# Attention and two feed-forward layers on one core: the first pass's input matmul in f16 parts, sums of |x| for the scales, one ring of streamed weights

## The chip, the core and the metric

The kernel runs on one core of a Trainium2 chip. The metric is device time in microseconds (us) of a whole execution. The engines are TensorE (PE, matmuls, with its weight loads PEld), VectorE (DVE), ScalarE (ACT), GpSimd (POOL), and the queue of SyncE (SP), which issues the DMA transfers. Each engine takes its instructions in program order, so an instruction that waits holds all that stand behind it on that engine.

## The reference

Four batches, eight heads, 576 positions and 64 dimensions a head give 2304 tokens of 512 columns. A position attends to all positions of its own and of earlier blocks of 64. Two feed-forward layers follow, 512 to 2048 to 512 columns, the first with h * tanh(softplus(h)) (Mish), the second with the square of relu.

```
attn = softmax(where(block_i >= block_j, q @ k.T / 8, -1e9));  x = attn @ v
h = x @ moe_w_in;   x = (h * tanh(log1p(exp(h)))) @ moe_w_out
h = maximum(x @ moe2_w_in, 0);   out = (h * h) @ moe2_w_out
```

## The kernel before

The tokens are cut into six chunks of 384. A pass is one layer of one chunk, and the twelve passes run in the order (layer, chunk) = (0,0), (0,1), (0,2), (1,0), (1,1), (0,3), (1,2), (1,3), (0,4), (0,5), (1,4), (1,5). The attention of a later chunk is laid beside the passes of earlier ones: `attention_lo` (chunks 0 and 1, f32 matmuls, tiles of 192) and `attention_hi` (chunks 2 to 5, f16 parts, scores at L903, maximum at L914, exponential at L925, product at L1011).

A pass takes eight weight pairs j, each two columns f of 128 hidden units. The first matmul of a column is four steps over the 512 inputs into one of two PSUM banks `hp`; ACT turns the bank into `h` with Mish or relu; `g_parts` (L1116 to L1118 the high part, L811 the low one) cuts g into two f16 parts; the second matmul adds into four banks `acc`. In most passes f32 is imitated by f16 parts: three f16 matmuls (high x high, low x high, high x low) for a step, in `first_half` (L1343) and `second_half` (L1456). Four passes go by a scheme of seven products (`first_seven`, L1376). All this needs the scale of a chunk's x (`chunk_scale`: one matmul at L1268 over per-token maxima `xm`, then operations on single columns that end in `cst`), the parts `xt` of x cut with it (L1276), and the norm and the parts of each weight pair (`decode` L1135 to L1146, `weigh` L1158 and L1161, `split` L1176). Pass (0,0) alone multiplies in f32, with `first_full` (L1407) and `second_full` (L1421). It needs no scale of x and no parts, only the decoded pairs; layer 0's w_in pairs are split later, out of the f32 pairs that lie in the buffer `first`.

The maxima of |x| that the scales start from are DVE reductions (L1028 in `settle`, L1428, L1473, L1550). Sums of absolute values are taken elsewhere, by `absum`, on ACT (L822) or DVE. An ACT function may need a table load first; the tasks carry a `table` by which the planner counts that, and those of `absum` carry none.

Layer weights that are not kept are written to `wspill` and read back by `weights` (L1246) into rings of buffers: `ws` up to pass 2, `wl` from pass 3, `wm` from pass 8. `wl` lies in the same memory as `ws`, and one line (L1747) makes its first three loads wait for all uses of `ws`:

```
    follow(R["wl"].insts[0:3], R["ws"].insts)
```

The order of the whole program is a table of numbers, `PLAN`, decoded by `Sched.planned`: for each place in the order it gives a task and the engine that runs it (tasks made by `choose` may run on one of several). The table was found by a search over a planner's estimates, and with the table the planner's estimates no longer matter.

## Time and profile before

| what | value |
|---|---|
| median of three runs | 898.1 us (894.83 to 899.0) |
| the profiled execution | 896.62 us, of which the span from first to last instruction is 894.8 |
| PE busy | 866.2 us, 97% |
| DVE busy | 766.5 us, 86% |
| ACT busy | 606.8 us, 68% |
| POOL busy | 54.2 us, 6% |
| first step on PE of passes 1 and 3 | 131.5 and 297.1 us |

The shares are means over the span. The windows of the section of rows cut it at the passes: a number in brackets there counts instructions, PEclk is the granted clock of TensorE as a share of full speed, and the DMA share is the mean busy share of the core's 16 DMA engines. A line such as L811 belongs to a helper and stands for several uses, told apart by the tile's name.

### The profile page before, as it was taken

The numbers are of one execution on the slowest core, as the hardware profiler recorded it, in microseconds if no ns is written. First come the engines' busy times: TensorE is split into PE (matmuls) and PEld (weight loads), VectorE is DVE, ScalarE is ACT, GpSimd is POOL, SyncE is SP. The second block draws the span as 40 slices with busy tenths as digits, with TensorE's granted clock in tenths as the row PEclk, the third lists the DMA queues.
The fourth block names the chain that finished last, engine by engine and source line by source line (L and its number), as shares of the span: only waits on it lengthen the run. The fifth ranks groups of instructions, "written<-read, shape, count | busy, mean of one in ns | idle before, by whom it ended". The sixth has DMA issues, their size and how long they took to land.

```text
span 894.8 us, 18486 instructions
## 1 busy us (share of the span) xinstructions
PE 866.2 (97%) x7034; PEld 600.7 (67%) x7034; DVE 766.5 (86%) x1816; ACT 606.8 (68%) x1157; POOL 54.2 (6%) x62
## 2 busy tenths in 40 slices
PE   7999999979999999999999999999999999999997
PEld 6664545545555456555556577777787877799997
DVE  6888988979989788886999899999887887689876
ACT  6799999899778675566678898975454333356332
POOL 1000100101110001000000000000010001010000
PEclk9999999999999999999999999999999999999999
DMA  9996676988798899588989699998569474766751
GB/s 340 362 354 263 167 158 174 246 260 292 250 300 206 187 242 224 180 195 216 218 261 277 244 215 264 257 236 319 196 247 335 162 287 173 257 215 236 249 200 59
DMA packets 162777, 213.02 MB, mean 238 GB/s; under 512 B 107392, under 2 KB 125824, under 8 KB 162688
## 3 DMA queue, kind: packets, MB, share of 16 engines
q1 hardware_dynamic: 162688, 211.84, 79.0%
q8 instruction: 55, 0.90, 0.4%
q14 instruction: 34, 0.28, 0.1%
...
## 4 chain that ended last, share of the span: by engine, by line
PE 71%; DVE 11%; ACT 9%; DMA 6%; issue 3%; SPq 0%; DVEq 0%; ACTq 0%
PE acc L1456 22%; PE hp L1376 15%; PE hp L1343 11%; PE acc L1496 4%; PE hp L1407 4%; PE acc L1421 3%; PE bank L903 3%; PE bank L1011 2%; DMA late<-pb 2%; DMA arena<-wspill 2%; PE bank L1496 2%; DVE st L914 1%; DVE pb L811 1%; ACT vs L822 1%; ACT pad L925 1%
## 5 line engine op out<-in xcount | busy, mean ns | idle before, releaser
L1456 PE MATMUL acc<-g,arena 128*128 128x384 f16 x1560 | 299.5, 326 | 0.1
L1456 PEld LDWEIGHTS <-arena 128*128 128x128 f16 x1560 | 147.2, 98 | 87.3 <-issue 4.6
L1343 PE MATMUL hp<-xt,first 128*128 128x384 f16 x576 | 111.3, 326 | 5.0 <-ACT h L1348 5.0
L1376 PEld LDWEIGHTS <-arena 128*128 128x128 f16 x1002 | 85.0, 98 | 13.5 <-DMA arena<-wspill 1.5
L1343 PEld LDWEIGHTS <-first 128*128 128x128 f16 x576 | 54.6, 98 | 44.8 <-issue 10.4
L811 DVE SCALAR_TENSOR_TENSOR g<-h,cst,g 128x768 f16<-128x768 f32 x72 | 73.2, 1017 | 3.1 <-ACT g L1116 2.5
L1343 PE MATMUL hp<-xt,arena 128*128 128x384 f16 x384 | 74.8, 332 | 0.9 <-DMA arena<-wspill 0.9
L925 ACT ACTIVATE pad<-bank,st,sq 128x448 f32<-128x448 f32 (+1 forms) x96 | 65.1, 681 | 13.9 <-DVE st L919 10.1
L811 DVE SCALAR_TENSOR_TENSOR pb<-pad,st,pb 128x384 f16<-128x384 f32 (+2 forms) x96 | 71.1, 749 | 2.6 <-ACT pb L945 2.5
L914 DVE TENSOR_REDUCE st<-bank 128x1 f32<-128x448 f32 (+1 forms) x96 | 53.2, 574 | 22.6 <-PE bank L906 14.4
L1348 ACT ACTIVATE h<-hp,cst 128x384 f32<-128x384 f32 x80 | 44.3, 576 | 29.6 <-PE hp L1343 28.9
L945 ACT ACTIVATE pb<-pad,st 128x640 f16<-128x640 f32 (+2 forms) x72 | 51.6, 725 | 14.6 <-DVE st L937 5.2
L1376 PEld LDWEIGHTS <-first 128*128 128x128 f16 x672 | 57.2, 98 | 5.2
L1376 PE MATMUL hp<-arena 128*128 128x192 f16 x534 | 55.2, 246 | 0.0
L1343 PEld LDWEIGHTS <-arena 128*128 128x128 f16 x384 | 36.7, 99 | 26.5 <-issue 2.8
L1397 ACT ACTIVATE h<-h,cst 128x576 f32<-128x576 f32 x32 | 24.7, 773 | 38.2 <-DVE h L1395 38.2
L1407 PE MATMUL hp<-xs,first 128*128 128x384 f32 x128 | 48.6, 492 | 1.0 <-ACT h L1411 1.0
L1376 PE MATMUL hp<-xt,arena 128*128 128x192 f16 x468 | 46.7, 246 | 1.2 <-DMA arena<-wspill 0.8
L1210 DVE TENSOR_TENSOR arena<-arena 128x256 f32<-128x256 f32 x96 | 40.6, 423 | 0.9
L903 PE MATMUL bank<-q 64*128 64x448 f16 (+2 forms) x384 | 39.3, 306 | 1.6 <-ACT xs L1025 0.7
L1116 ACT ACTIVATE g<-h,cst 128x768 f16<-128x768 f32 x36 | 33.5, 930 | 9.9 <-PE acc L1456 7.6
L1421 PE MATMUL acc<-h,late 128*128 128x384 f32 x96 | 37.4, 495 | 0.0
...
## 6 DMA issues: line engine op xcount, KB each, us to landing
...
arena<-in_w_dram SPq DMA_DIRECT2D x27, 1023.8 KB, 6.5
...
```

Source lines behind the costliest of these rows:

```text
L811: return sch.add("DVE", c_dve(n) + 62 * ap, lambda: nc.vector.scalar_tensor_tensor(dst(), a(), s() if ap else s, c(), op0, op1), r=r, w=w, ...
L903: nc.tensor.matmul(out=pp.t[hd][:, o:o + k1 - k0], lhsT=qh.t[rows, u, a:a + 128], rhs=qh.t[rows, w, nq + k0:nq + k1], start=p == 0, stop=p ...
L914: t = sch.add("DVE", c_dve(o1 - o0), lambda hd=hd: nc.vector.reduce_max(st.t[:, 2 * j + hd:2 * j + hd + 1], pp.t[hd][:, o0:o1], axis=AX.X) ...
L925: t = sch.add("ACT", c_act(o1 - o0, True, 3), lambda hd=hd: nc.scalar.activation(pf[hd].t[r0:, k0:k0 + o1 - o0], view(hd)[r0:, o0:o1], AF. ...
L945: "ACT": ("ACT", c_act(n, False, 1), lambda pb=pb, pv=pv, s=s: nc.scalar.activation(pb.t[:, 0:i + 1, 0, :], pv(), AF.Copy, scale=s()), False),
L1343: nc.tensor.matmul(out=hp.t[:, 0:n], lhsT=w.t[:, f % 2, a, 128 * k:128 * k + 128], rhs=x.t[:, c, k, 0:n], start=k == 0 and i == 0, stop=k ...
L1348: sch.add("ACT", c_act(n, True, 1), lambda f=f, o=o, hp=hp: nc.scalar.activation(h.t[:, o * n:o * n + n], hp.t[:, 0:n], (AF.Mish, AF.Relu) ...
L1376: nc.tensor.matmul(out=bank.t[:, o:o + z], lhsT=lhs, rhs=x.t[:, c, ks[k], :], start=start and k == 0 and i == 0, stop=k == 1 and i == 2, s ...
L1407: nc.tensor.matmul(out=hp.t[:, 0:n], lhsT=wf.t[:, 512 * (f % 2) + 128 * k:512 * (f % 2) + 128 * k + 128], rhs=xs.t[:, k, 0:n], start=k == ...
L1421: ts.append(sch.add("PE", c_mm(4 * n), lambda m=m, acc=acc: nc.tensor.matmul(out=acc.t[:, 0:n], lhsT=wf.t[:, 512 * (f % 2) + 128 * m:512 * ...
L1456: nc.tensor.matmul(out=acc.t[:, 0:n], lhsT=wo.t[:, f % 2, a, 128 * m:128 * m + 128], rhs=g.t[:, c, f % 2 * n:f % 2 * n + n], start=f == 0 ...
L1496: nc.tensor.matmul(out=acc[bank].t[:, o:o + c1 - c0], lhsT=lhs, rhs=g.t[:, c, z * b + c0:z * b + c1], start=j == 0 and (bank, o) in first ...
```

## The change

The first two weight pairs of pass (0,0) keep the f32 matmul (`NFULL` is 2); pairs 2 to 7 go through `first_half` with f16 parts. So chunk 0's x gets a scale and parts as well, in the buffer that chunk 2 uses later, and each w_in pair of layer 0 is normed by itself. The pairs from the third on are decoded into the ring `wf` of two buffers and split from there; the first two lie in the last two places of `first`. The rules that held a split back until the f32 readers were done are gone.

All maxima become `absum`, sums of |x|, in f32, on ACT or DVE; chunk 0 gets them too. `absum` tells the planner that it wants ACT's exponential table. The rings `ws` and `wl` become one, `ws`, used up to pass 7, and the line that made the first loads wait goes. The table `PLAN` is another one. Its order has 49 ACT table loads where the old has 58; 16 f32 steps of the first matmul in pass 0 where the old has 64; 26 norm matmuls (L1161) where there were 20, and 12 scale matmuls (L1268) where there were 11. Of the 56 sums of x 36 are on ACT and 20 on DVE, where 48 maxima were on DVE; DVE gets 24 more operations on single columns.

```diff
-X_AT = {(0, 1): "b", (0, 2): "c", (0, 3): "a", (0, 4): "y", (0, 5): "z",
+X_AT = {(0, 0): "c", (0, 1): "b", (0, 2): "c", (0, 3): "a", (0, 4): "y", (0, 5): "z",
...
-    "c-mE(34o8){{KJc`95YC!!UMHghWcHt0<L7`@SmIEvYL-S4pc#H>p%N+GtND>8DMLXc5`>-56sDV;{y?X3Y8gU*|l}^PT=pGxPmE=bX>^tnc^dGhZS`YDzOX"
...
+    "c-l>x2Vhji*2mB6-XydTO6Wz3C;}oXqJj-ju>gt)=zEGNs3<5RJXBEZiYWNm6%kQEd?<EQ#QGGF-g^(dg-$5RobNX?_Xb#Yv$=QX%qjo#Kj-X5q@1YcNL?w?"
...
-    R["wl"] = fixed([pair(arena[:, 1024 * i:1024 * i + 1024]) for i in range(3)])
...
     for j in range(NF // 2):
-        R["f32", 0, j] = fixed([first[:, 1024 + 2048 * j:3072 + 2048 * j].bitcast(F32)])
+        if j < NFULL:
+            R["f32", 0, j] = fixed([first[:, 2048 * (j + NF // 2 - NFULL):2048 * (j + NF // 2 - NFULL + 1)].bitcast(F32)])
         R["res", 0, 0, j] = fixed([first[:, 2048 * j:2048 * j + 2048].rearrange("p (a f c) -> p f a c", a=2, f=2)])
...
-    R["xm"] = sb("xm", [128, 8], BF16, 12)
+    R["xm"] = sb("xm", [128, 8], F32, 5)
+    junk = cp.tile([128, NX], BF16, name="junk")
+
+    nbytes[0] += 2 * NX
...
-    R["cst"] = sb("cst", [128, 37], F32, 4)
+    R["cst"] = sb("cst", [128, 37], F32, 3)
...
-    for key, old, more in (("wm", "wl", [pair(late[:, 0:1024]), pair(late[:, 1024:2048]), pair(vst[:, 1536:2560])]),
+    for key, old, more in (("wm", "ws", [pair(late[:, 0:1024]), pair(late[:, 1024:2048]), pair(vst[:, 1536:2560])]),
...
     def absum(n, total, src, spare, r, w):
...
-            "DVE": ("DVE", c_dve(n), lambda: nc.vector.tensor_reduce(total(), src(), axis=AX.X, op=ALU.add, apply_absolute_value=True), False)}, r, w)
+            "DVE": ("DVE", c_dve(n), lambda: nc.vector.tensor_reduce(total(), src(), axis=AX.X, op=ALU.add, apply_absolute_value=True), False)}, r, w).table = "exp"
...
-        xs, xm, whole = xs
+        xs, xm = xs
         dst = lambda: xs.t[:, k, xo:xo + n]
...
-        if not whole:
-            sch.add("DVE", c_dve(n), lambda: nc.vector.tensor_reduce(
-                xm.t[:, j:j + 1], dst(), axis=AX.X, op=ALU.max, apply_absolute_value=True), r=[(xs, (k, xo))], w=[(xm, j)])
+        absum(n, lambda: xm.t[:, j:j + 1], dst, lambda: junk[:, 0:n], [(xs, (k, xo))], [(xm, j)])
...
-    halves_of, used = {}, {}
...
     def decode(l, k, j):
 
         sch.group = "decode", l, k, j
         raw = R["raw2" if l else "raw"].new()
-        wf = (R["f32", k, j] if l == 0 else R["wf"]).new()
+        wf = R["wf" if l or not k and j >= NFULL else ("f32", k, j)].new()
...
-        if (l, k) == (0, 0):
-            hi = [t for t in w.tasks if t not in lo]
-            lo[0].deps.update(hi)
-            halves_of[j] = hi, lo
         if (k, j) in RES[l]:
...
-            w = fetched[pi, l, k, j] = R["wm" if pi >= WM_AT else "wl" if pi >= WL_AT else "ws"].new()
+            w = fetched[pi, l, k, j] = R["wm" if pi >= WM_AT else "ws"].new()
...
-    def chunk_scale(l, xs, xm, x, n, m, at, first, seven, lone):
+    def chunk_scale(l, xs, xm, x, n, m, at, seven, lone):
...
-        step = sch.add("PE", 120.0, lambda: nc.tensor.matmul(out=sc.t[:, 0:m], lhsT=ones, rhs=xm.t[:, 0:m], start=True, stop=True), r=[xm], w=[sc])
+        step = sch.add("PE", 120.0, lambda: nc.tensor.matmul(out=sc.t[:, 0:m], lhsT=ones, rhs=upper(xm.t[:, 0:m]), start=True, stop=True), r=[xm], w=[sc])
...
-        def spread():
-            for a, b in [(2 * j, 2 * j + 2) for j in range(NF // 2)] if first else [(0, NF)]:
+        def spread(j=None):
+            for a, b in [(0, NF) if j is None else (2 * j, 2 * j + 2)]:
                 tiny(lambda a=a, b=b: nc.vector.tensor_scalar(c(HS + a, b - a), st.t[:, IN + a:IN + b], c(PX), 0.25, ALU.mult, ALU.mult),
                      [(cst, PX)] + [(st, (0, j)) for j in range(a // 2, b // 2)], [(cst, (HS, j)) for j in range(a // 2, b // 2)], b - a)
...
-                sch.add("DVE", c_dve(n), lambda m=m, o=o: nc.vector.tensor_reduce(
-                    xm.t[:, m:m + 1], o(), axis=AX.X, op=ALU.max, apply_absolute_value=True), r=[(xs, (m, 0))], w=[(xm, m)])
+                absum(n, lambda m=m: xm.t[:, m:m + 1], o, lambda: junk[:, 0:n], [(xs, (m, 0))], [(xm, m)])
...
                 if l == 0:
-                    sch.add("DVE", c_dve(n), lambda m=m, o=o: nc.vector.tensor_reduce(
-                        xm.t[:, m:m + 1], o(), axis=AX.X, op=ALU.max, apply_absolute_value=True), r=dst, w=[(xm, m)])
+                    absum(n, lambda m=m: xm.t[:, m:m + 1], o, lambda: junk[:, 0:n], dst, [(xm, m)])
...
-                sch.add("DVE", c_dve(n), lambda m=m: nc.vector.tensor_reduce(
-                    xm.t[:, m:m + 1], y.t[:, m, 0:n], axis=AX.X, op=ALU.max, apply_absolute_value=True), r=r, w=[(xm, m)])
+                absum(n, lambda m=m: xm.t[:, m:m + 1], lambda m=m: y.t[:, m, 0:n], lambda: junk[:, 0:n], r, [(xm, m)])
...
+        xs, xm = whole(A_SLOT[c]), R["xm"].new()
         begin = len(sch.tasks)
-        place(chunk_steps(c, (xs, xm, c == 0), c < 2), a, b)
+        place(chunk_steps(c, (xs, xm), c < 2), a, b)
...
-    wfs, wos, m1s, hs = [], [], [], []
+    sch.group = "scale", 0, 0
+    x0, cst0, _, spread0, _, _ = chunk_scale(0, *source[0, 0], halved(X_AT[0, 0]), n, 8, A_AT[0][1], False, False)
+    sch.group = None
+    wfs, wos, hs, us0 = [], [], [], []
     for j in range(NF // 2):
         wfs.append(decode(0, 0, j))
         wos.append(decode(0, 1, j))
-        hs.append(R["h"].new())
+        us0.append(weigh(0, 0, [j], [wfs[j]], S_AT[0][0] + j * S_AT[0][1]))
+        if j < NFULL:
+            hs.append(R["h"].new())
+            m1 = [t for f in (2 * j, 2 * j + 1) for t in first_full(f, n, xs, wfs[j], hs[j])]
+            m1[0].mark = (0, 0) if j == 0 else None
+        else:
+            split(0, 0, j, wfs[j], us0[j], 0)
+            sch.group = "scale", 0, 0
+            spread0(j)
+            sch.group = None
+            m1, h = first_half(0, 0, j, n, x0, cst0)
+            hs.append(h)
         for f in (2 * j, 2 * j + 1):
-            m1 = first_full(f, n, xs, wfs[j], hs[j])
-            m1[0].mark = (0, 0) if f == 0 else None
-            m1s.append(m1)
-            put(m1)
+            put(m1[f % 2 * KC:f % 2 * KC + KC])
             if f >= FLAG:
                 put(second_full(f - FLAG, n, hs[(f - FLAG) // 2], wos[(f - FLAG) // 2], state))
+        if j == NFULL:
+            for i in range(NFULL):
+                split(0, 0, i, wfs[i], us0[i], 0)
     for f in range(NF - FLAG, NF):
         put(second_full(f, n, hs[f // 2], wos[f // 2], state))
     for j0 in range(0, NF // 2, NGRP):
         js = list(range(j0, j0 + NGRP))
-        us = [weigh(0, k, js, [(wfs, wos)[k][j] for j in js], S_AT[k][0] + js[-1] * S_AT[k][1]) for k in (0, 1)]
+        us = weigh(0, 1, js, [wos[j] for j in js], S_AT[1][0] + js[-1] * S_AT[1][1])
         for j in js:
-            for k in (0, 1):
-                split(0, k, j, (wfs, wos)[k][j], us[k], j - j0)
+            split(0, 1, j, wos[j], us, j - j0)
...
-    for j in range(NF // 2):
-        readers = [t for f in (2 * j, 2 * j + 1) for t in m1s[f]]
-        hi, lo = halves_of[j]
-        for t in lo:
-            t.deps.update(readers)
-        if j + 1 < NF // 2:
-            for t in halves_of[j + 1][0]:
-                t.deps.update(readers + lo + hi)
...
-    follow(R["wl"].insts[0:3], R["ws"].insts)
...
-    follow(R["u"].insts[0:2], R["f32", 0, NF // 2 - 1].insts)
+    for j in range(NFULL):
+        follow([here[0, 0, NF // 2 - NFULL + j]], R["f32", 0, j].insts)
...
-    carry("wm", "wl")
+    carry("wm", "ws")
...
-WL_AT, WM_AT = 3, 8
+WM_AT, NFULL = 8, 2
...
-S_AT = [[45190.0, 3570.0], [18510.0, 2110.0]]
+S_AT = [[19000.0, 8000.0], [38510.0, 4110.0]]
```

The first place is DVE in pass 0, beside the attention of chunk 1. `first`, `arena` and `pad` hold weights in the making, `us` and `wst` their scales and norms, `st` softmax statistics, `xm` per-token maxima. Before:

```order
L1118 TENSOR_SCALAR first<-first,us_420 128x1024
L1055 TENSOR_REDUCE st_663<-bank_124 128x1
L1056 TENSOR_SCALAR st_663<-st_663 128x3
L1054 TENSOR_REDUCE st_672<-bank_123 128x2
L1146 SCALAR_TENSOR_TENSOR first<-arena,pad 128x1024
L1028 TENSOR_REDUCE xm_538<-xs 128x1
L1055 TENSOR_REDUCE st_672<-bank_123 128x1
L1056 TENSOR_SCALAR st_672<-st_672 128x3
L811 SCALAR_TENSOR_TENSOR first<-first,us_420 128x1024
```

After, at about the same count of DVE instructions (`cst_607` is chunk 0's scale, `xt` its parts):

```order
L1109 TENSOR_SCALAR cst_607<-cst_607 128x1
L1113 TENSOR_SCALAR us_416<-wst_485 128x1
L1146 CAST pad<-arena 128x1024
L1113 TENSOR_SCALAR cst_607<-cst_607 128x1
L1147 SCALAR_TENSOR_TENSOR arena<-arena,pad 128x1024
L790 COPY pt<-bank_124 128x448
L1168 TENSOR_SCALAR wst_485<-bank_125 128x2
L815 SCALAR_TENSOR_TENSOR xt<-xs,cst_607,xt 128x384
```

The scale of chunk 0's x and its low part have come into DVE's row here. On PE 162 of the 176 attention matmuls of `attention_lo` and 25 steps of pass 0 stand ahead of the first f16 step; at that point of attention the old order had 32 steps.

The second place is the queue SP before pass 3. `wspill_63` holds layer 0's spilled weights and `wspill_64` layer 1's; L950 (L954 after) are attention's transposes. Before:

```order
L1246 DMA arena<-wspill_63 128x2048
L950 DMA_TRANSPOSE late<-pb 128x6x128
L1191 DMA wspill_64<-arena 128x2048
L866 DMA vs<-in_va_dram 128x640
L950 DMA_TRANSPOSE late<-pb 128x6x128
L1246 DMA arena<-wspill_64 128x2048
L950 DMA_TRANSPOSE late<-pb 128x8x128
L1246 DMA arena<-wspill_64 128x2048 x2
L950 DMA_TRANSPOSE late<-pb 128x8x128
L1246 DMA arena<-wspill_64 128x2048
```

After:

```order
L1136 DMA arena<-in_w_dram 128x4095
L1243 DMA arena<-wspill_64 128x2048
L954 DMA_TRANSPOSE late<-pb 128x6x128
L870 DMA vs<-in_va_dram 128x640
L954 DMA_TRANSPOSE late<-pb 128x6x128
L1188 DMA wspill_64<-arena 128x2048
L954 DMA_TRANSPOSE late<-pb 128x8x128
L869 DMA qk<-in_qp_dram 128x960
L1243 DMA arena<-wspill_63 128x2048
L954 DMA_TRANSPOSE late<-pb 128x8x128
L1243 DMA arena<-wspill_64 128x2048
```

Before, the loads of layer 1 all stand behind the last load of layer 0, and the first of them waits for the ring; after, one stands seven places ahead of that last load, and more follow it. On PE, 48 second matmuls of pass 2 stand behind the first step of pass 3 in the new order; in the old one all of them stood ahead of it.

## Rows read from the trace of the kernel before

**Rows 1.** Windows, one per stretch; columns in the first line; x counts instructions
```profile
core 0: us, PE busy (x) PEld busy (x) DVE busy (x) ACT busy (x) POOL busy (x), PEclk, DMA share, GB/s
0.00:31.60 31.60, 26.28 (x183) 21.78 (x184) 22.66 (x88) 22.65 (x90) 3.72 (x13) 1.00 0.94 342
31.60:131.40 99.80, 96.91 (x427) 55.72 (x426) 86.17 (x210) 91.80 (x188) 2.97 (x3) 1.00 0.80 260
131.40:217.70 86.30, 79.68 (x569) 45.60 (x568) 76.64 (x182) 79.89 (x135) 8.48 (x9) 1.00 0.83 235
217.70:297.00 79.30, 75.59 (x510) 43.50 (x507) 71.75 (x168) 61.29 (x104) 9.82 (x11) 1.00 0.81 243
297.00:652.00 355.00, 350.17 (x2801) 224.82 (x2802) 313.63 (x762) 253.26 (x494) 16.51 (x15) 1.00 0.88 234
652.00:894.80 242.80, 237.59 (x2553) 209.24 (x2550) 195.62 (x414) 97.95 (x149) 12.68 (x11) 0.99 0.63 221
```

**Rows 2.** PE timeline, passes 0 and 1: start us, us, what, count
```profile
121.65 0.81 PE L1421 MATMUL acc<-h,late 128*128 128x384 f32 x2
...
122.29 0.81 PE L1421 MATMUL acc<-h,arena 128*128 128x384 f32 x2
...
131.50 0.65 PE L1343 MATMUL hp<-xt,first 128*128 128x384 f16 x3
...
137.28 1.63 PE L1343 MATMUL hp<-xt,first 128*128 128x384 f16 x9
...
138.74 0.81 PE L1421 MATMUL acc<-h,arena 128*128 128x384 f32 x2
```

**Rows 3.** PE timeline, in the early attention of pass 0
```profile
61.45 1.51 PE L1407 MATMUL hp<-xs,first 128*128 128x384 f32 x4
```

**Rows 4.** Windows from the start, columns as in rows 1
```profile
0.00:62.00 62.00, 56.68 (x320) 41.15 (x321) 48.61 (x146) 48.76 (x150) 3.72 (x13) 1.00 0.95 358
...
0.00:124.20 124.20, 116.93 (x563) 73.74 (x563) 104.39 (x279) 107.33 (x267) 6.69 (x16) 1.00 0.83 286
...
0.00:286.60 286.60, 270.40 (x1625) 162.21 (x1626) 248.09 (x614) 250.78 (x502) 24.24 (x35) 1.00 0.84 262
```

**Rows 5.** Groups by line and shape, DVE: count, busy, mean ns, idle
```profile
L811 DVE SCALAR_TENSOR_TENSOR xt<-xs,cst,xt 128x384 f16<-128x384 f32 x14 | 8.9, 648 | 0.0
...
L1028 DVE TENSOR_REDUCE xm<-xs 128x1 bf16<-128x384 f32 x16 | 8.4, 547 | 0.0
```

**Rows 6.** Groups by line and shape, ACT
```profile
L822 ACT ACT_TABLE_LOAD x9 | 11.5, 1283 | 0.2
...
L822 ACT ACTIVATE vs<-qk 128x384 f16<-128x384 f32 x11 | 5.7, 518 | 1.8 <-PE bank L1011 1.8
```

**Rows 7.** PE timeline, from pass 2 into pass 3
```profile
293.49 0.17 PE L1161 MATMUL bank<-us,onesq 128*128 128x1 bf16 x1
...
297.14 5.75 PE L1343 MATMUL hp<-xt,arena 128*128 128x384 f16 x24 [0.86 <-DMA arena<-wspill]
```

**Rows 8.** Timeline of the DMA queue SP, same place
```profile
293.69 0.33 SPq L1246 DMA_DIRECT2D arena<-wspill  x1
```

**Rows 9.** Windows behind the start of pass 3
```profile
296.00:300.00 4.00, 3.14 (x19) 1.55 (x14) 3.24 (x18) 2.02 (x5) 0.00 (x0) 0.72 1.07 245
300.00:304.00 4.00, 4.00 (x25) 1.95 (x24) 1.33 (x5) 2.72 (x8) 0.00 (x0) 0.85 0.83 180
```

**Rows 10.** Waits of PE, 132 to 218: total us, times, longest
```profile
PE hp L1343 <- ACT h L1348: 4.1, 2, 2.7
```

**Rows 11.** ACT timeline within pass 1
```profile
182.52 1.28 ACT L822 ACT_TABLE_LOAD   x1
...
185.16 1.28 ACT L1348 ACT_TABLE_LOAD   x1
...
186.46 0.58 ACT L1348 ACTIVATE h<-hp,cst 128x384 f32<-128x384 f32 x1
```

**Rows 12.** The page's DMA issues: KB each, median us to landing
```profile
arena<-in_w_dram SPq DMA_DIRECT2D x27, 1023.8 KB, 6.5
```

More of the change, by code (lines that the diff above doesn't have):

```diff
@@ new lines @@
+    "^Vq+Oj=ThHa2EHSC-Sum=dJ}kOIeZ6{YAdA)x)j>;MaX-wGFHGP&b@iHStLy=hZ-;>dZf9QZ){vL1p7APH9=@vt=DJ79nFbvU7=g0~jMi%HhRJB!!QQ@IWEw"
+    "6@ilFSa3q!WOD+{Eo9db{CtGm+=A~*k;!GG1fI;o8~gF~F|c$1_HdKfOk^B@7qa|!rk0BFCv`G~FTSE493_KRiL0_{B4o*(0<c;Nj1(bxEL^aRQ~!;e<8%TA"
+    "`klwkVQSk}?tcj?3OLctk}u<#;q3fge#ifNKu89&TP9QIE;RTQyA1wHA=!N%Ze%0=a^I4!!c#~6w~yGv^90%Bz6(vkWc&QLs43R$)tA_R9Bs-VDVKFKiNGOh"
+    "R}Oy5!`5taX+1JGlKZ>x?JlhTgEcMLcaSrbymt{VWX(J*JqAuJOjXx^u6UeN50afO-oh1k@)cM&mOIYtMZCHR{3!3|Q`6_M=a}9CU*%!*dak%{)AHffwe+OB"
@@ L1593, in attention @@
     def attention(c, a, b):
-        xs, xm = whole(A_SLOT[c]), R["xm"].new() if c else None
+        xs, xm = whole(A_SLOT[c]), R["xm"].new()
         begin = len(sch.tasks)
-        place(chunk_steps(c, (xs, xm, c == 0), c < 2), a, b)
+        place(chunk_steps(c, (xs, xm), c < 2), a, b)
         for t in sch.tasks[begin:]:
@@ L1603, in tile_attention_moe, with scale @@
     ready, due = {}, []
-    def scale(l, c, m, at, first=False):
+    def scale(l, c, m, at):
         sch.group = "scale", l, c
@@ L1608, in scale @@
         x = (summed if seven else halved)(X_AT[l, c])
-        x, cst, norm, spread, rest, later = chunk_scale(l, *source[l, c], x, n, m, at, first, seven, lone)
+        x, cst, norm, spread, rest, later = chunk_scale(l, *source[l, c], x, n, m, at, seven, lone)
         if l == 0:
```

179 lines of the change are left out of this document (88 added, 91 removed).

## The prediction

> **What bounds the kernel now.** I read the stretches of the program first, one per pass [rows 1]. From 297 us on TensorE (PE) is busy for 350.2 of 355.0 us, and from 652 us for 237.6 of 242.8: there nothing but PE's own work counts. Before 297 us PE idles 5.3 us up to 31.6, then 2.9, 6.6 and 3.7 us in the three passes that follow, and VectorE (DVE) and ScalarE (ACT) are nearly as full: in pass 0 after 31.6 us ACT is busy 91.8 and DVE 86.2 of 99.8 us. So the first 297 us are a race of three engines, and an edit is worth there what it takes off the engine that is last. The change lies almost wholly there. The profiled execution took 896.6 us; the median of the runs is 1.5 us above it, inside their spread, and I sum against 896.6.
>
> **Term 1: first matmul of pass 0 in f16.** An f32 step takes 0.645 us (121.65 to 122.29); nine f16 matmuls take 1.46 us (137.28 to 138.74), so the three that replace an f32 step take 0.487 [rows 2]. By the orders of instructions 48 of 64 steps change: 48 x 0.158 = 7.6 us less on PE. Six more norm matmuls and one more scale matmul at about 0.03 us each give 0.2 back. **-7.4 us.** In passes 1 and later the multiplier is the same, so nothing follows there.
>
> **Term 2: what the f16 steps must wait for.** An f32 step needs x and a weight pair; an f16 step needs chunk 0's scale, x cut into two f16 parts, and the pair normed and split as well. PE runs in order, so behind the first f16 step stand pass 0's second matmuls and all of chunk 1's attention, with the maxima on DVE and the exponentials on ACT that wait for its scores. At the same point of attention PE has done 25 matmul steps in the new order where it had 32 by 61.45 us [rows 3]: 7 x 0.645 = 4.5 us less, so PE is there at 56.9. DVE has 48.5 us of work ahead of x's first lo part in the new order (its instructions counted, each at its mean); in the old one it had done as much at 62.0 us [rows 4]. A first wait of 5.1 us follows. At the other end, DVE has 7.4 us more work ahead of pass 1's x: 113.2 us, against 105.8 (both counted at the means), which the old order reached at 124.2; the trace itself has 104.4 busy there [rows 4]. The four lo parts of chunk 0's x are 4 x 0.648 = 2.6 us of that [rows 5]; the weight splits that stood later are most of the rest. So x comes at 124.2 + 7.4 = 131.6 us, while PE, 7.4 us lighter, would be there at 131.5 - 7.4 = 124.1 (131.50 is pass 1's first f16 step in [rows 2]). PE waits for all it has gained. The bounds: 0, if the added DVE work falls into DVE's idle time, 19.8 us before 124.2 [rows 4]; +7.4, if none does. I take the upper, since at 62.0 us DVE already idles 13.4 us in waits that the new order does not shorten (the DMA engines are busy 0.95 of it). **+7.4 us.** The weights of six pairs now pass through two buffers, so decoding pair j waits for the split of pair j-2; a raw transfer that starts too late for that would cost up to 6.5 us [rows 12] once, which the range's upper end takes in.
>
> **Term 3: one ring of weights.** Before, the loads for pass 3 go to buffers that are free only when every load of the old ring has been read. PE ends pass 2's second matmul at 293.49, the load is issued at 293.69 [rows 8], and the first f16 step starts at 297.14 [rows 7], 3.45 us later; 0.86 of it is charged to the transfer. In the new order the queue SP issues layer-1 loads between the last layer-0 ones, and 48 second matmuls of pass 2 stand behind pass 3's first step, so PE has work while a load is late. Bounds 0.86 and 3.45; between the ends lie some scores that wait for DVE and would remain. I take 2.6, nearer the upper, since with matmuls behind the first step those scores are no longer all that PE has. In addition the granted clock falls to 0.72 in 296 to 300 and 0.85 in 300 to 304 [rows 9], right after that idle: between the two levels of 1.2 and 2.4 GHz, 4 x 0.28 + 4 x 0.15 = 1.7 us, which goes if PE stays busy. **-4.3 us** (bounds 0 and -5.2).
>
> **Term 4: table loads and token sums.** The orders show 49 table loads on ACT instead of 58, mostly in front of Mish in pass 0 and of the exponentials. They cost ACT, and reach PE only where it waits for Mish: in pass 1 that is 4.1 us in two waits [rows 10]. In that pass the count goes from 14 to 12. Around 185 us two loads of 1.28 us stand ahead of one Mish [rows 11]; one less is **-1.3 us** (bounds -2.6 and +2.6, two loads fewer or two more in front of a Mish that PE waits for). The token sums: 48 maxima at 0.547 us on DVE [rows 5] become 20 sums there and 36 on ACT, at 0.518 us for the same width [rows 6] and its accumulator read. Neither engine has to finish a sum before PE's next step except at a pass's start, where the scale needs it; DVE's relief of 28 sums x 0.547 = 15.3 us lies mainly after 297 us, where PE hides it, and I cost it at nothing. If that cover failed it would be a gain. The 24 added operations on single columns are inside term 2's count.
>
> Here a rule speaks against the edit. The rows show nine table loads at the line of Abs, 1.283 us each [rows 6]. The Trainium skill, "ScalarE: Activation LUTs", section "Table sets: the hidden batching unit", says that cheap functions such as abs are in every set; by that an Abs would never need a load, and giving it a table in the search would bring nothing, 892.3 in place of the sum below. These rows contradict it. The same page, section "What ACT_TABLE_LOAD costs", puts a switch at 2.66 us with a drain; by that, term 4 would be -2.7 and the sum 889.6. In the trace the load at 185.16 ends at 186.44 and the Mish starts at 186.46 [rows 11], with no drain to be seen.
>
> **Sum:** 896.6 - 7.4 + 7.4 - 4.3 - 1.3 = 891.0 us.
>
> **Rivals.**
> A, the forecast, 891.0; its own range is 887 to 895, by term 3's and term 4's bounds. Chance 0.42.
> B, DVE keeps ahead: term 2 is 0 and f16's gain stays, 896.6 - 7.4 - 4.3 - 1.3 = 883.6. For it: DVE idles 13.6 us between 31.6 and 131.4 us [rows 1], more than the 7.4 added, and the sums moved to ACT relieve it. Against: ACT is fuller still there (91.8 of 99.8). Chance 0.22.
> C, the gain at the ring dissolves: PE's wait for the load becomes a wait for DVE's g, of which those 48 second matmuls are made. DVE has 71.8 of 79.3 us in pass 2 [rows 1], and the new order puts 4 to 8 us more DVE work ahead of pass 2's end. Term 3 is 0 and only term 4 stays: 895.3. Chance 0.22.
> D, slower: DVE sets the pace from the first f16 step to the end of pass 2. It is busy 248.1 of 286.6 us [rows 4]. If its 38.5 us of idle time do not shrink, because they come from waits in the chain scale, parts, matmul, Mish, g, the 7.4 us stay on the end of pass 2 without PE's gain to pay for them, and terms 3 and 4 are hidden behind DVE: 896.6 + 7.4 = 904.0. It decides from the point at which DVE starts pass 1's x later than 131.6 us. Chance 0.14.
> That the change does not do what it says is excluded for the matmuls and the loads, which the orders show; it is open only in what they bring.
>
> **How the numbers follow.** A comparison of this kernel can tell about 0.5% from no change, 893.6 to 902.6 us around 898.1. A lies mostly below (0.31 of 0.42), B wholly (0.22); C is nearly all inside, A's rest and a part of D too; D otherwise above. Faster 0.54, same 0.34, slower 0.12. The range reaches from B's 884 to 900, past C's 895.3 by the bounds of terms 2 to 4, and leaves D and the extremes out.
>
> **What would show it.** Right, if in the new profile PE's first f16 step in pass 0 comes near 62 us after a wait of about 5 us for x's parts from DVE; if pass 1 starts at 131 to 132 us; if pass 3's first f16 step starts with no wait for a weight load and the granted clock stays at 1.0 there; and if the stretches after it are as long as before. Pass 1 at 124 to 127 us means B. A pass 3 that starts at 297 us or a little before, with PE waiting for g or scores from DVE, means C. Pass 1 later than 132 us, with DVE idle as long as before, means D. The forecast is wrong at its root if the order from 297 us on, which I left at no change, brings waits of its own on ACT, where the 36 sums now stand among the exponentials.

## The result, and the profile after

The changed kernel takes 873.6 us (median of four runs, 872.96 to 874.18), the kernel before 896.5 us (median of four). The ratio is 0.9744, 95% interval 0.9712 to 0.9776: 22.9 us faster. The forecast was 891.0, range 884 to 900, so the sign was right and the time lies 10 us below the range. The profiled execution of after took 873.4 us with a span of 871.6.

PE's first step of each pass shows where the 23.2 us of the span went. Passes 2 and 3 are taken together, because 48 matmuls were moved from the one into the other.

| stretch | before, us | after, us | difference |
|---|---|---|---|
| up to pass 0 | 31.6 | 33.0 | +1.4 |
| pass 0 | 99.8 | 89.7 | -10.1 |
| pass 1 | 86.3 | 80.7 | -5.6 |
| passes 2 and 3 | 152.7 | 145.6 | -7.1 |
| passes 4 to 11, to the last matmul | 518.8 | 517.1 | -1.7 |

The first row is not told from the scatter between executions: in the profiles of the old order's variants below, whose work up to there is that of before, pass 0 starts between 31.6 and 33.4 us.

The windows of after, cut at the same places as [rows 1] (busy us of PE, PEld, DVE, ACT, POOL, then granted clock, DMA share, GB/s):

```profile
0.00:33.00 33.00, 27.68 (x185) 22.65 (x186) 24.93 (x90) 25.66 (x101) 1.95 (x11) 1.00 0.95 352
33.00:122.70 89.70, 89.39 (x481) 51.60 (x480) 87.31 (x227) 86.31 (x191) 7.58 (x7) 1.00 0.79 266
122.70:203.40 80.70, 79.30 (x568) 45.26 (x567) 77.23 (x187) 76.50 (x140) 7.43 (x8) 1.00 0.95 268
203.40:269.40 66.00, 66.00 (x453) 38.46 (x452) 62.28 (x150) 60.50 (x104) 9.82 (x9) 1.00 0.90 279
269.40:628.50 359.10, 356.74 (x2865) 228.51 (x2864) 313.15 (x765) 254.11 (x510) 30.72 (x30) 1.00 0.88 235
628.50:871.60 243.10, 237.44 (x2548) 208.83 (x2546) 193.02 (x406) 97.53 (x152) 21.16 (x16) 0.99 0.62 218
```

In pass 0 PE now idles 0.3 us (2.9 in [rows 1]), DVE 2.4 us (13.6) and ACT 3.4 us (8.0). All three engines are full at once. That DVE would stay idle was the base of the forecast's term 2. On PE, around the first f16 step of pass 0 (start us, us, engine, line, operation, count):

```profile
58.64 0.22 PE L1052 MATMUL bank<-never,above 128*128 128x128 bf16 x1
58.70 0.65 PE L1340 MATMUL hp<-xt,first 128*128 128x384 f16 x3
59.19 1.45 PE L1418 MATMUL acc<-h,late 128*128 128x384 f32 x4
```

It comes with no wait. On DVE, the first low part of x:

```profile
55.59 0.77 DVE L815 SCALAR_TENSOR_TENSOR xt<-xs,cst,xt 128x384 f16<-128x384 f32 x1
```

The window up to the first f16 step (DVE is the third busy time):

```profile
0.00:58.70 58.70, 53.38 (x310) 39.26 (x311) 49.85 (x155) 50.97 (x163) 4.00 (x13) 1.00 0.95 364
```

The low part ends at 56.4 us; I had put it at 62.0. PE is there at 58.7, 1.8 us later than I had it. The waits of PE in pass 1 (engine, line, released by, us in total, times, longest), beside the 4.1 us for Mish of [rows 10]:

```profile
PE bank L881 <- ACT vs L826: 0.6, 1, 0.6
PE bank L1162 <- ACT wsq L1159: 0.4, 1, 0.4
PE bank L1162 <- ACT tl L788: 0.2, 1, 0.2
```

No wait for Mish is left. ACT's table loads by line (count, busy us, mean ns, idle before), where Mish is L1345 and L1408, the exponential L929, and the sums L826:

```profile
L1345 ACT ACT_TABLE_LOAD x20 | 25.7, 1283 | 1.2 <-PE hp L1340 0.9
L929 ACT ACT_TABLE_LOAD x12 | 15.4, 1283 | 0.2
L826 ACT ACT_TABLE_LOAD x11 | 14.1, 1283 | 0.2
L1408 ACT ACT_TABLE_LOAD x2 | 2.6, 1283 | 0.0
```

Counted by pass, passes 0, 1 and 2 have 11, 12 and 8 loads where before had 17, 14 and 11: 11 loads, 14.1 us of ACT, fewer: six in pass 0, two in pass 1, three in pass 2. At the place of [rows 7 to 9], the passage from pass 2 to pass 3, PE weaves second matmuls (L1452) into the first steps of pass 3 (`hp<-xt,arena`), and the granted clock stays up:

```profile
268.56 0.65 PE L1452 MATMUL acc<-g,arena 128*128 128x384 f16 x3
269.05 0.65 PE L1340 MATMUL hp<-xt,first 128*128 128x384 f16 x3
269.53 0.65 PE L1340 MATMUL hp<-xt,arena 128*128 128x384 f16 x3
```
```profile
266.00:270.00 4.00, 4.00 (x30) 2.08 (x28) 3.64 (x10) 2.60 (x5) 0.00 (x0) 1.00 1.08 280
270.00:274.00 4.00, 4.00 (x33) 2.42 (x32) 2.94 (x9) 2.57 (x6) 0.91 (x1) 1.00 1.04 236
```

### The profile page after: what moved, and what is told of

It reads as the page before. It is cut to its first block, busy times and chain, and to the rows that moved or that the text cites. A ratio compares the mean times of both kernels' runs of the same rounds, so it can differ in the third digit from the quotient of the medians.

```text
span 871.6 us, 18660 instructions
## 1 busy us (share of the span) xinstructions
PE 856.5 (98%) x7089; PEld 595.3 (68%) x7089; DVE 757.9 (87%) x1822; ACT 600.6 (69%) x1194; POOL 78.7 (9%) x80
## 4 chain that ended last, share of the span: by engine, by line
PE 73%; ACT 11%; DVE 11%; DMA 3%; issue 2%; SPq 0%; DVEq 0%; ACTq 0%
PE acc L1452 24%; PE hp L1340 15%; PE hp L1373 15%; PE acc L1491 4%; PE acc L1418 3%; PE bank L907 3%; DMA arena<-wspill 2%; ACT pad L929 2%; PE bank L1015 1%; PE bank L1491 1%; PE hp L1404 1%; DVE st L918 1%; ACT L1345 1%; DVE g L815 1%; ACT h L1345 1%
## 5 line engine op out<-in xcount | busy, mean ns | idle before, releaser
L1452 PE MATMUL acc<-g,arena 128*128 128x384 f16 x1560 | 300.1, 326 | 0.0
L1452 PEld LDWEIGHTS <-arena 128*128 128x128 f16 x1560 | 147.3, 98 | 85.1 <-issue 2.9
L1340 PE MATMUL hp<-xt,first 128*128 128x384 f16 x720 | 139.8, 326 | 0.2
L1340 PEld LDWEIGHTS <-first 128*128 128x128 f16 x720 | 67.9, 98 | 52.0 <-issue 9.5
L1373 PEld LDWEIGHTS <-arena 128*128 128x128 f16 x1002 | 84.7, 98 | 14.9 <-DMA arena<-wspill 2.3
L1345 ACT ACTIVATE h<-hp,cst 128x384 f32<-128x384 f32 x92 | 51.2, 578 | 37.0 <-PE hp L1340 34.9
L1340 PE MATMUL hp<-xt,arena 128*128 128x384 f16 x384 | 72.8, 326 | 0.2 <-DMA arena<-wspill 0.2
L929 ACT ACTIVATE pad<-bank,st,sq 128x448 f32<-128x448 f32 (+1 forms) x96 | 65.1, 681 | 10.1 <-DVE st L923 4.9
L1373 PEld LDWEIGHTS <-first 128*128 128x128 f16 x672 | 57.3, 98 | 5.0 <-issue 0.3
L949 ACT ACTIVATE pb<-pad,st 128x640 f16<-128x640 f32 (+2 forms) x70 | 49.3, 720 | 10.9 <-DMA late<-pb 4.0
L1340 PEld LDWEIGHTS <-arena 128*128 128x128 f16 x384 | 35.9, 98 | 24.8 <-issue 1.1
L1119 POOL TENSOR_SCALAR g<-h,cst 128x768 f16<-128x768 f32 x18 | 20.0, 1110 | 233.7 <-ACT h L1345 63.4
L1390 ACT ACTIVATE h<-hp,cst 128x192 f32<-128x192 f32 x32 | 13.4, 420 | 36.4 <-PE hp L1373 35.9
L1491 PEld LDWEIGHTS <-arena 128*128 128x128 f16 x504 | 37.6, 98 | 0.1
```

The costliest lines, as they stand in the source:

```text
L929: t = sch.add("ACT", c_act(o1 - o0, True, 3), lambda hd=hd: nc.scalar.activation(pf[hd].t[r0:, k0:k0 + o1 - o0], view(hd)[r0:, o0:o1], AF. ...
L949: "ACT": ("ACT", c_act(n, False, 1), lambda pb=pb, pv=pv, s=s: nc.scalar.activation(pb.t[:, 0:i + 1, 0, :], pv(), AF.Copy, scale=s()), False),
L1340: nc.tensor.matmul(out=hp.t[:, 0:n], lhsT=w.t[:, f % 2, a, 128 * k:128 * k + 128], rhs=x.t[:, c, k, 0:n], start=k == 0 and i == 0, stop=k ...
L1345: sch.add("ACT", c_act(n, True, 1), lambda f=f, o=o, hp=hp: nc.scalar.activation(h.t[:, o * n:o * n + n], hp.t[:, 0:n], (AF.Mish, AF.Relu) ...
L1373: nc.tensor.matmul(out=bank.t[:, o:o + z], lhsT=lhs, rhs=x.t[:, c, ks[k], :], start=start and k == 0 and i == 0, stop=k == 1 and i == 2, s ...
L1452: nc.tensor.matmul(out=acc.t[:, 0:n], lhsT=wo.t[:, f % 2, a, 128 * m:128 * m + 128], rhs=g.t[:, c, f % 2 * n:f % 2 * n + n], start=f == 0 ...
```

## The experiments

The experiments keep one of the two orders and change the work of one engine in it, or the place of a few tasks; the last two take the order away. Where a task had to wait for something new, it was put back by as little as that demands. Line numbers shift by a few lines from kernel to kernel.

### PE's work, in the old order and in the new

Twelve f32 steps left out of pass 0 in the old order:

```diff
         def mm1(k):
+            if f >= 4 and k == KC - 1:
+                return
...
```

> The kernel before, leaving out the last of four f32 steps of the first matmul in pass 0 for twelve of sixteen columns: 12 x 0.645 = 7.7 us less PE work, the amount that the f16 steps save, in the old order; the output is not the reference's. Theory 1 (PE sets the pace of pass 0 in the old order too, so the f16 gain is a gain by itself): 7 to 8 us faster. Theory 2 (ACT and DVE set the pace of passes 0 to 2 in the old order, and only the new order makes PE the last): 0 to 3 us faster, with more idle time on PE before 297 us.

Measured: 896.2 us against 897.6 for before, ratio 0.9986 (0.9964 to 1.0007). Windows of passes 0 and 1:

```profile
31.90:131.00 99.10, 90.71 (x403) 51.24 (x402) 85.57 (x208) 90.69 (x187) 2.98 (x3) 1.00 0.79 262
131.00:219.70 88.70, 81.43 (x570) 46.19 (x569) 77.95 (x183) 80.95 (x136) 9.07 (x9) 0.98 0.85 232
```

PE has 6.2 us less to do in pass 0 than in [rows 1] and the pass is 0.7 us shorter: PE idles 8.4 us instead of 2.9. Theory 2 holds for the old order. The same amount added in the new order:

```diff
             def mm1(k, f=f, w=w, hp=hp):
+                for _ in range(4 if pi == 0 and k == 0 else 0):
+                    nc.tensor.matmul(out=hp.t[:, 0:n], lhsT=w.t[:, f % 2, 0, 0:128], rhs=x.t[:, 0, 0, 0:n], start=True, stop=True)
```

> The kernel after, with 48 more f16 matmuls in pass 0 (four more at the first step of each of twelve columns, overwritten by the real ones): 48 x 0.162 = 7.8 us more PE work, so the first matmul of pass 0 costs what it cost in f32; the order and all else is as after. Theory 1 (in the new order PE is last in pass 0, so the f16 gain is whole): 7 to 8 us slower than the kernel after. Theory 2 (the gain came from ACT and DVE): 0 to 3 us slower than it.

Measured: 880.95 us (879.2 to 881.9), 7.3 more than after. Pass 0:

```profile
33.30:130.40 97.10, 97.03 (x529) 56.31 (x528) 87.86 (x228) 87.25 (x192) 7.57 (x7) 1.00 0.74 247
```

PE takes all of it and idles 0.1 us. The price of an f16 step in term 1 was right, and of the two orders only the new one turns it into time.

### Table loads, put in and taken out

Six one-column exponentials ahead of six Mish operations in the new order:

```diff
+                    if len(extra) % 2: nc.scalar.activation(junk[:, 0:1], ones[:, 0:1], AF.Exp)
```

> The kernel after, with six one-column exponentials put ahead of six Mish operations in passes 0 to 2, so that ACT loads tables 12 times more often (61 loads; before had 11 more than after in these passes): 12 x 1.28 = 15.4 us more on ACT and some 0.5 us for the small operations. Theory 1 (the table loads that the new order avoids are most of the gain that the forecast did not see): 8 to 15 us slower than after. Theory 2 (ACT has room for them, 13 us of idle time in passes 0 to 2): 0 to 4 us slower.

Measured: 896.1 us (891.9 to 898.8), 22.5 more than after, nearly the whole gain. Theory 1, and more than its upper figure. ACT at one of the places, then the windows of passes 0 and 1, the waits of PE in them, and a window behind the place:

```profile
129.42 1.28 ACT L1793 ACT_TABLE_LOAD   x1
130.72 0.21 ACT L1793 ACTIVATE junk<-ones 128x1 bf16<-128x1 bf16 x1
130.94 1.28 ACT L1345 ACT_TABLE_LOAD   x1
132.23 0.58 ACT L1345 ACTIVATE h<-hp,cst 128x384 f32<-128x384 f32 x1
```
```profile
33.20:132.70 99.50, 92.40 (x481) 52.30 (x479) 88.10 (x228) 94.60 (x198) 7.57 (x7) 0.98 0.73 245
132.70:224.90 92.20, 83.64 (x566) 46.98 (x567) 78.52 (x190) 85.57 (x150) 7.42 (x8) 0.94 0.81 241
...
132.00:136.00 4.00, 3.13 (x7) 1.61 (x7) 1.61 (x2) 3.97 (x7) 0.00 (x0) 0.59 0.61 242
```
```profile
PE hp L1340 <- ACT h L1345: 6.0, 3, 2.6
PE hp L1302 <- ACT h L1345: 3.0, 1, 3.0
```

Twelve loads are 15.4 us. In the trace six fall into pass 0, which then has 17, as before had, and six into pass 1, which has 18, more than before's 14. Pass 0 is 9.8 us longer and so as long as before's (99.5 us against 99.8); pass 1 is 11.5 us longer. Of these 21.3 us 14.0 are idle time of PE, with waits for Mish that after did not have, and 7.3 are PE's own work taking longer: the granted clock is 0.59 right behind an idle stretch and 0.94 over pass 1. So more than the loads' own time is lost. The control puts squares in the same places, which need no table:

```diff
-                    if len(extra) % 2: nc.scalar.activation(junk[:, 0:1], ones[:, 0:1], AF.Exp)
+                    if len(extra) % 2: nc.scalar.activation(junk[:, 0:1], ones[:, 0:1], AF.Square)
```

> The kernel after with the six one-column operations of the earlier run put in at the same places, but squares instead of exponentials, which need no table: 49 table loads, as after. If the table loads were what cost 22.5 us there, this is within 1 us of after; if the added instructions disturbed the order, several us slower.

Measured: 873.8 us (873.4 to 874.8), as after. It is the loads. With both the loads and the added matmuls:

> The kernel after with both additions: the six exponentials that bring 12 more table loads (alone 22.5 us slower than after) and the 48 f16 matmuls that give pass 0 its f32 price back (alone 7.3 us slower). Theory 1 (with the loads on ACT, PE is no longer last in pass 0, so its work is free there, as the left-out steps were in the old order): within 3 us of the kernel with the loads alone. Theory 2 (the two are separate prices): 6 to 8 us slower than that one, some 30 us slower than after.

Measured: 897.7 us (894.3 to 899.8), 1.6 more than with the loads alone, and the two ranges overlap; the matmuls alone cost 7.3. Pass 0 in its profile:

```profile
34.00:137.30 103.30, 98.92 (x529) 57.20 (x527) 88.36 (x228) 94.69 (x199) 7.56 (x7) 0.98 0.72 236
```

With 12 more loads on ACT, most of PE's saving is gone in the new order as well: pass 0 is 3.8 us longer than with the loads alone, and pass 1 is 1.7 us shorter. Now the other way, in the old order: sums of absolute values that ACT takes while Mish's table is loaded go to DVE.

```diff
+            if name == "ACT" and t.mark == "abs" and table == "mish":
+                name = "DVE"
+            table = name == "ACT" and t.table or table
```

> The kernel before in its own order, with nine sums of absolute values that ACT took while Mish's table was loaded given to DVE: 46 table loads instead of 58, so 15.4 us of loads and about 6 us of sums less on ACT, and nine sums of 0.4 to 0.8 us more on DVE. Theory 1 (ACT with its table loads sets the pace of passes 0 to 2 in the old order; twelve loads put into the new order cost 22.5 us): 8 to 20 us faster than before. Theory 2 (the gain is the new order's finer placing, the loads only hurt where they were put): 0 to 4 us faster, with DVE taking over as the last.

Measured: 889.4 us against 897.9, ratio 0.9905 (0.9880 to 0.9930): 8.4 us faster, the lower end of theory 1. Passes 0 and 1:

```profile
33.40:129.90 96.50, 96.23 (x427) 55.87 (x426) 88.08 (x212) 85.68 (x177) 2.98 (x3) 1.00 0.81 267
129.90:210.80 80.90, 79.73 (x570) 45.67 (x569) 78.40 (x187) 71.50 (x122) 8.49 (x9) 1.00 0.91 251
```

Of the twelve loads four each were in pass 0, pass 1 and pass 5. Pass 1 takes 80.9 us, as in after (80.7), though its order is the old one: this edit alone brings 5.4 us there, and after gained 5.6. It does so with ten loads where after has twelve, and with sums off ACT too, so that loads made the 5.6 us of after is not shown. Pass 0 gains 3.3, where after gained 10.1, and PE is then busy for 96.2 of its 96.5 us. Then with the twelve f32 steps left out as well:

> The kernel before with both edits: nine sums of absolute values moved from ACT to DVE (46 loads) and the last of four f32 steps left out for twelve columns of pass 0 (7.7 us less PE work; the output is not the reference's). The left-out steps alone gave 1.3 us. Theory 1 (the f16 gain needs ACT to be relieved first): 5 to 8 us faster than with the moved sums alone. Theory 2 (in the old order something else, DVE, holds pass 0 once ACT is relieved): within 2 us of it.

Measured: 888.2 us (885.5 to 891.0), 1.3 less than with the moved sums alone: theory 2. Pass 0 and its last 26.8 us:

```profile
31.80:126.80 95.00, 90.17 (x403) 51.38 (x402) 87.17 (x211) 84.48 (x176) 2.98 (x3) 1.00 0.81 268
```
```profile
100.00:126.80 26.80, 25.43 (x124) 13.89 (x124) 25.21 (x64) 25.66 (x44) 2.98 (x3) 1.00 0.78 200
```

In the old order PE's saving is still idle time (4.8 us) once ACT has 7 us less to do. From 100 us on PE, DVE and ACT are each busy for 25.2 to 25.7 of 26.8 us, so that none of them alone is seen to hold the others there. That the order of their work is what keeps the saving from counting is an inference; which part of the order, no run shows. In the new order the same sort of edit, six sums between two Mish operations to DVE (43 loads instead of 49):

> The kernel after in its own order, with the six sums of absolute values that ACT takes between two Mish operations given to DVE: 43 table loads instead of 49, 7.7 us of loads and some 4 us of sums less on ACT, six sums of about 0.6 us more on DVE. The same edit in the old order gave 8.4 us for twelve loads. Theory 1 (ACT is still last in passes 0 and 1): 3 to 6 us faster than after. Theory 2 (PE is last there now, as the added matmuls showed): within 1.5 us of after.

Measured: 874.7 us (874.0 to 875.5), 1.1 more than after: theory 2. The run speaks for less than was meant, since in its trace only two of the six loads are gone from pass 1 and none from pass 0. In pass 1 ACT is no longer last (81.2 us, 80.7 in after); for pass 0 it is the added matmuls that show PE last.

### Sums of x on ACT

```diff
             name = ("PE", "ACT", "DVE", "POOL", "SP")[raw[2 * n + i]]
+            if t.group == "xsum":
+                name = "DVE"
```

> The kernel after in its own order, with the 36 sums of x that ACT takes given to DVE: 36 x 0.33 to 0.55 us, some 18 us, more on DVE, which is 97% busy in pass 0 after, and some 25 us less on ACT, with three table loads fewer. Theory 1 (the moved sums matter: DVE is close to the last engine too): 5 to 15 us slower than after. Theory 2 (only ACT's table loads matter, the sums are hidden): within 3 us of after.

Measured: 880.7 us (880.5 to 880.8), 7.1 more than after. Passes 0 and 1:

```profile
33.20:125.00 91.80, 90.31 (x481) 51.55 (x480) 88.74 (x234) 84.30 (x177) 7.57 (x7) 1.00 0.78 260
125.00:206.10 81.10, 79.23 (x568) 45.27 (x567) 78.98 (x192) 74.05 (x130) 7.42 (x8) 1.00 0.98 268
```

2.1 us of it lie in pass 0, 0.4 in pass 1, and 2.3 in the first of the seven-product passes (77.2 us instead of 74.9). The sums are not hidden, as term 4 had them; in this order 36 of them on ACT are worth some 7 us, with three table loads to pay for.

### f32 throughout pass 0, in the new order

```diff
-            m1, h = first_half(0, 0, j, n, x0, cst0)
-            hs.append(h)
+            hs.append(R["h"].new())
+            m1 = [t for f in (2 * j, 2 * j + 1) for t in first_full(f, n, xs, wfs[j], hs[j])]
```

> The kernel after in its order, with all of pass 0's first matmul in f32 again; scale, parts and splits of pass 0 stay. The pairs from the third on are in the ring of two buffers, so a pair's decoding now waits until the f32 steps of the pair two before it are done, and 72 instructions move back for that. The f16 steps alone account for 7.6 us, as the added matmuls showed. Theory 1 (the early split frees the buffers and that matters as much as PE's time): 12 to 25 us slower than after. Theory 2 (only PE's time matters): 6 to 9 us slower.

Measured: 935.7 us (933.3 to 937.1), 62 more than after; neither theory came near. Pass 0, and PE's main waits in it:

```profile
33.10:181.40 148.30, 112.25 (x433) 62.53 (x432) 89.68 (x225) 87.07 (x188) 4.12 (x6) 0.84 0.50 164
```
```profile
PE bank L1179 <- ACT wsq L1176: 17.0, 5, 4.6
PE bank L924 <- ACT pad L946: 12.3, 6, 5.2
```

With f32 steps reading the pairs, a buffer comes free only when they are done, decoding waits, and the norm matmuls on PE wait for that. The granted clock is 0.84 over the pass. This speaks for the two-buffer ring being workable because the f16 split empties a buffer early. But the run also moves 72 instructions back, and how much of the 62 us that costs is not shown.

### The rings and the passage from pass 2 to pass 3

The old ring's wait narrowed to the loads that used the same memory:

```diff
-    follow(R["wl"].insts[0:3], R["ws"].insts)
+    for i in range(3):
+        follow(R["wl"].insts[i:i + 1], R["ws"].insts[i::3])
```

> The kernel before, with one edit: each of the first three loads of the second ring waits only for the loads that used its own third of the memory, not for all uses of the first ring. The order of instructions is as before. Theory 1 (the wait at the ring costs what the forecast's term 3 says): pass 3 starts without PE waiting for the load, the granted clock stays up, and the time falls by 2.6 to 5.7 us. Theory 2 (the wait passes on to the next late thing, scores or the g of pass 2): less than 1.5 us. The new kernel lost 5.7 us less in pass 2 than the old one.

Measured: 896.3 us, ratio 0.9987 (0.9972 to 1.0001). On SP the load was still issued when pass 2 had ended:

```profile
294.15 0.32 SPq L1246 DMA_DIRECT2D arena<-wspill  x1
```

Its third of the memory was one that the last load had used, so the run does not test the wait. It shows something else: PE waits 1.33 us for that load, more than in [rows 7], and the granted clock stays up behind it, where before's profile has 0.72 and 0.85 [rows 9]:

```profile
296.00:300.00 4.00, 2.67 (x26) 1.65 (x25) 3.07 (x17) 1.21 (x3) 0.00 (x0) 1.00 1.05 218
300.00:304.00 4.00, 4.00 (x29) 2.17 (x28) 2.31 (x6) 4.00 (x10) 0.00 (x0) 1.00 1.18 278
```

So the fall of the clock there is no fixed price of a late load. One ring instead, in the old order:

```diff
-            w = fetched[pi, l, k, j] = R["wm" if pi >= WM_AT else "wl" if pi >= WL_AT else "ws"].new()
+            w = fetched[pi, l, k, j] = R["wm" if pi >= WM_AT else "ws"].new()
```

> The kernel before with after's one ring of weights instead of two. The ring hands out its buffers in the order of use, so in the old order 30 instructions that now have to wait for a load issued later are put behind it, among them second matmuls of pass 2, which so come behind pass 3's first load; nothing else moves. Theory 1 (what the new kernel saves at the end of pass 2 is the overlap of the two passes that one ring allows, not the wait at the old one): 3 to 6 us faster than before. Theory 2 (it is the new order's placing of the work of ACT and DVE through pass 2): within 2 us of before.

Measured: 905.2 us, ratio 1.0090 (1.0053 to 1.0126), slower. The second matmuls that were put behind pass 3's first load wait for their own, later load:

```profile
PE acc L1472 <- DMA arena<-wspill: 7.9, 1, 7.9
```

One ring is no gain by itself; it needs an order of loads to go with it. Next, both rings, with the buffers taken in the order in which they come free and the load three places earlier on SP:

```diff
...
+        rank[self.load] = rank[self.last] + 0.5
...
```

> The kernel before with the second ring's buffers taken in the order in which the first ring's come free, each load waiting for its own buffer alone, and the first load of pass 3 issued three places earlier on SP, ahead of a load of v and two transposes; PE's order is as before. Theory 1 (PE's wait for that load is what pass 2 loses at its end): 3 to 5 us faster. Theory 2 (in the old order scores that wait for DVE stand between the passes, so an early load only moves the wait): 0 to 2 us faster, with PE idle before the scores as it was.

Measured: 895.3 us, ratio 0.9981 (0.9958 to 1.0004). The load is issued at 284.8 us and PE's wait for it is gone; what is left before pass 3's first step is scores that wait for DVE:

```profile
296.13 0.31 PE L921 MATMUL bank<-q 64*128 64x320 f16 x1 [0.61 <-DVE q L908]
296.75 0.29 PE L921 MATMUL bank<-q 64*128 64x320 f16 x1 [0.31 <-DVE sv L850]
...
298.17 2.11 PE L1361 MATMUL hp<-xt,arena 128*128 128x384 f16 x12
```

Passes 2 and 3 take 150.0 us in its profile, 2.7 less than before, not told from no change in the whole. Here they are in before, with the narrowed wait, with the early load, and in after:

```profile
217.70:370.40 152.70, 148.47 (x1037) 85.28 (x1034) 131.46 (x324) 106.99 (x207) 14.82 (x15) 0.99 0.83 229
218.40:369.60 151.20, 146.87 (x1036) 84.73 (x1033) 131.55 (x324) 107.06 (x207) 14.82 (x15) 1.00 0.85 229
219.80:369.80 150.00, 146.54 (x1036) 84.58 (x1033) 131.00 (x323) 106.69 (x207) 14.82 (x15) 1.00 0.85 232
203.40:349.00 145.60, 145.40 (x1036) 83.81 (x1035) 127.12 (x323) 110.01 (x213) 17.73 (x16) 1.00 0.84 239
```

PE idles 4.2, 4.3, 3.5 and 0.2 us. The early load takes 0.8 us of idle time away; the other 1.9 are PE's work taking less time at a clock that did not fall, and 1.6 of these the narrowed wait has too, with the load as late as before. Then pass 3's first eight steps between the last eight of pass 2:

```diff
...
+        for a, b in zip(self.m2, self.m1):
+            rank[b] = rank[a] + 0.5
...
```

> The same, and the eight steps of pass 3's first pair now stand among the last eight second steps of pass 2, ahead of the scores, instead of behind them. Theory 1 (the gain at this place is overlap of the two passes, which a load that is early enough permits): 3 to 6 us faster than before, no idle time of PE between the passes, granted clock 1.0. Theory 2 (the 5.8 us are lost all through pass 2, to ACT and DVE): 0 to 2 us faster.

Measured: 899.9 us, ratio 1.0029 (1.0005 to 1.0054). The norm matmuls now stand later on PE, DVE waits for them, and PE waits for DVE's low part of x and for ACT after that:

```profile
298.60 0.23 DVE L1187 TENSOR_SCALAR wst<-bank 128x2 uint32<-128x2 uint32 x2 [2.59 <-PE bank L1181]
```
```profile
302.46 0.81 PE L1363 MATMUL hp<-xt,arena 128*128 128x384 f16 x4 [1.19 <-DVE xt L831]
304.18 0.35 PE L923 MATMUL bank<-q 64*128 64x448 f16 x1 [0.90 <-ACT pad L945]
```

And with nine sums moved to DVE as well:

> The kernel before with that edit and with the nine sums of absolute values moved from ACT to DVE (12 table loads fewer, alone 8.4 us). If the two gains lie at different places they add: 11 to 15 us faster than before. If both relieve the same wait: 8 to 10 us.

Measured: 891.7 us, ratio 0.9931 (0.9903 to 0.9958), less of a gain than with the moved sums alone.

### Both kernels without their searched order

```diff
-PLAN = (
...
+PLAN = ""
```

> The kernel before with its table of the order taken out: the planner's own forward pass sets the order from its estimates (76 table loads). It serves as the other side of the next kernel, after's parts with no search. I expect it slower than before by 2 to 8%.

> The kernel after with its table of the order taken out, ordered by the same forward pass (75 table loads). Theory 1 (the gain is mostly the searched order, which ACT's loads and idle times follow; the edits to the code bring little by themselves): within 1% of the kernel before without its table, 0 to 8 us faster. Theory 2 (the edits bring the 23 us whatever the order): 15 to 30 us faster than that one.

Measured: 1017.2 us (1015.2 to 1019.4) for before's parts, 1011.3 us (1007.7 to 1013.7) for after's: 5.9 us apart. The 13% was more than I had guessed. Under the planner's own pass the edits are worth 0.6%, and its loads do not fall (76 and 75). The order found by search is worth some 120 us to the one and 138 to the other. So most of the 22.9 us came with the searched order; what a search would have found for one of the edits without the others, no run shows.

## Why the prediction failed, step by step

**What bounds the kernel.** Right in that the first 297 us are a race of three engines and that all but 1.7 us of the change lie ahead of pass 4; wrong in taking DVE for the engine that would be last. In the old order 6.2 us less on PE shorten pass 0 by 0.7 us, and fewer loads and sums on ACT shorten it by 3.3 and pass 1 by 5.4. That ACT had this hold is seen from the runs and not from the busy times: in pass 0 PE paused less (96.9 us busy of 99.8, ACT 91.8), in pass 1 both were equally full (79.7 and 79.9 of 86.3) [rows 1], and in the last third of pass 0 of before both hardly paused:

```profile
100.00:131.40 31.40, 30.47 (x141) 16.57 (x140) 26.27 (x67) 30.25 (x55) 2.97 (x3) 1.00 0.78 191
```

**Term 1** was right in size: forecast -7.4 us, and adding the same work back in the new order costs 7.3.

**Term 2** failed: +7.4 forecast, 0 or less measured. The step was "in waits that the new order does not shorten". DVE's 13.4 us of idle time up to 62.0 us became 8.9 up to the first f16 step at 58.7, and 13.6 became 2.4 in pass 0; the first f16 step came without the wait of 5.1 us. Pass 1 starts at 122.7 us; rival B had 124.1. A shortage of DVE was inferred from the time at which the old order had done as much work, and that time holds the old order's waits. The sums that went to ACT, which term 4 put at nothing, are part of DVE's room: back on DVE they cost 7.1 us, 2.1 of them in pass 0 and more than half after 297 us, where PE was to hide them.

**Term 3** was too small, and that it came within 3 us was luck, since the runs do not bear out its mechanism. Passes 2 and 3 together lost 7.1 us, against 4.3 forecast with -5.2 as the bound. Of the 2.6 us for the wait the early load gives 0.8 of PE's idle time in the profile and nothing that can be told in the time; the 1.7 us for the clock were a fall that need not come with the late load. Overlapping the two passes in the old order gave a loss of 2.8 us, but there the norm matmuls came later too. Moving the sums or the loads of the first passes leaves the gain where it is: the two passes take 145.4 to 146.8 us in the profiles of all three of these kernels in the new order (loads added, sums on DVE, f32) and 150.0 with the early load, 153.9 and 155.5 with the woven steps in the old order. What in the new order takes the other 3.3 us of PE's idle time, and the 1.1 us of PE's busy time by which after lies below the early load, is **open**.

**Term 4** was mis-sized, -1.3 us. The step was "reach PE only where it waits for Mish". By it the six loads fewer in pass 0 were put at nothing; put back in the new order they cost 9.8 us there. Pass 1 gave 5.6 us, though only two of its loads are gone; how much of that is loads is open. A load delays every ACT task behind it, and DVE and PE wait for such tasks, so a named wait of PE can be the last link only; that chain is a reading, not traced link by link. In the new order twelve loads cost 22.5 us: they also take away most of the f16 gain and let the clock fall.

**The sum** treated the terms as separate. In the new order they are not: PE's work put back costs 7.3 us, the loads 22.5, both together 24.1. PE's saving counts only where ACT has fewer loads, and in an order made for that: in the old order the saving gave 1.3 us, the loads and sums 8.4, both together 9.7, so that there the loads did not free it. Rival B had the mechanism of pass 0 and a chance of 0.22, but its 883.6 us still lacked the price of the loads. The later passes, left at no change, gained 1.7 us.

On the page that spoke against the edit ("ScalarE: Activation LUTs" of the Trainium skill, "Table sets: the hidden batching unit"): the runs stand against it. There are table loads in front of Abs in both kernels, and giving nine Abs to DVE took twelve loads away. Whether the set lacks Abs or the load is placed all the same, no run shows. The loads of the added exponentials show no drain either: 1.28 us at 130.94, and the Mish at 132.23.
